# Where an attention group stands among the FFN matmuls of TensorE: behind a second one rather than behind a first

## The chip, the cores and the metric

The kernel runs on one core of a Trainium2 chip. The metric is the device time of one execution in microseconds. The other cores are idle. Some executions take about 195 us instead of 189; they are called slow and left out of every comparison of times.

## The reference

A polysketch attention feeds an FFN with squared ReLU. Cut to what matters:

```python
# q, k, v: (4, 4, 1088, 32) f32;  S1, S2: (8, 32);  w_in: (128, 2048);  w_out: (2048, 128)
def phi(x):                                   # 64 features per position
    a, b = S1 @ x, S2 @ x                     # "sketch", 8 + 8
    return outer(a, b)
kv, z = sum_s phi(k) v, sum_s phi(k)          # per batch and head
x = (phi(q) @ kv) / (phi(q) @ z + 1e-6)       # -> (4 * 1088, 128)
h = max(x @ w_in, 0)                          # first FFN matmul, "mm1"
out = (h * h) @ w_out                         # second FFN matmul, "mm2"
```

## The kernel before

The order of the instructions on each engine is made on the host by a small list scheduler. Each operation has a key (lower is more urgent), the engines that can do it with an estimated duration, and what it depends on. The FFN operations are chained so that they alternate, `mm2(u)`, `mm1(u+4)`, `mm2(u+1)`, and so on; the attention groups of TensorE are put in when they are the most urgent one that is ready.

```python
    def run(self, hop=0.25):
        ...
        t = 0.0
        while todo:
            later, done = [], []
            for e in free:
                ...
                best, wait = None, []
                for op in todo:
                    ...                                   # r: when op is ready for e
                    if r > t:
                        later.append(r)
                        wait.append((r, op["key"]))
                    elif best is None or op["key"] < best["key"]:
                        best = op
                ...
                if best is not None:
                    best["start"], best["eng"] = t, e
                    ...
        for op in sorted(self.ops, key=lambda op: (op["start"], op["n"])):
            op["emit"](op["eng"])
```

What the groups and the FFN matmuls are on TensorE (names as the profile shows them):

```python
    # mm1, "pg<-xT,w_in": F32R, 128x128 of the array, ONE instruction of n columns
    nc.tensor.matmul(st["pg", u][:, n*i : n*i+n], w_in[:, 128*(d0+i) : ...], st[b, "xT"][:, c0 : c0+n])
    # mm2, "po<-g,w_o": f32, 128x128 of the array, TWO instructions of n columns
    nc.tensor.matmul(po[0][:, 0:n], w, g, start=(d == 0), stop=(d == NB - 1))

    # "qc", "kc" (the sketches): 16 tiles of 32x32, f32, so 32 instructions
    def sketch(t_, src, c0, n, w, col=0):
        for h in range(H):
            for c in range(4):
                r = slice(32*h, 32*h + 32)
                nc.tensor.matmul(t_[32*c : 32*c+32, 512*h+col : ...], w[r, :], src[r, c0+n*c : ...])
    # "kvp" (a_kvs): tiles of 128x32, 80 instructions;  "nd" (a_nd): tiles of 32x32, 64 instructions (in batch 0, 16 more of 128x32)
```

## Time and profile before

| | before |
|---|---|
| time, median of 6 runs | 189.32 us (189.06 to 195.55, one slow) |
| span of the profiled run | 187.4 us |
| TensorE on the chain that ended last | 94% |
| busy: PE, PEld, DVE, ACT | 97%, 65%, 61%, 80% |
| waits of TensorE's matmuls after 14.2 us | none listed |
| FFN pair with 384 columns | 0.82 us |

TensorE is the bound, so all that counts is how much time its own instructions take in their order. The useful measure of that is start to start. One caution for reading the timelines: within the steady alternation a pg is recorded as started about 0.3 us before its turn, while the second half of a po still streams (halves of a po start 0.32 us apart; the second half at 64.86 us streams until 65.18, and the next pg is recorded at 64.89). Recorded durations overlap, and only distances between like places are safe. The marks at both ends of what the change can reach, in the timeline of the kernel before, are the first FFN matmul and the last second one (columns: start, duration, engine, line, operation, operands, shape, count):

```profile
14.17 0.47 PE L615 MATMUL pg<-xT,w_in 128*128 128x256 f32 x2 [0.27 <-DVE xT L810]
...
182.28 1.06 PE L648 MATMUL pol<-w_o,g 128*128 128x128 f32 x8
```

They lie 182.28 - 14.17 = 168.11 us apart.

### The profile page before, as it was taken

The page shows a single profiled execution, that of the slowest core. Times are in us where ns is not written, and L with a number is a line of the kernel's source. Part 1 is how long each engine was busy: PE and PEld are TensorE (multiplying, and loading weights), DVE is VectorE, ACT ScalarE, POOL GpSimd, SP SyncE. Part 2 cuts the span into 40 slices and gives each one's busy share as a digit, 9 for nine tenths or more (in the row PEclk, how much of TensorE's full clock was granted, in tenths as well). Part 3 has the DMA queues.
Part 4 walks back from the last instruction along what each step waited for, and adds up shares of the span by engine and source line. Part 5 has one row for each costly group of instructions (what it writes and reads, how often), then busy time and mean ns, then how long its engine had stood idle before and what let it go on. Part 6 is the DMA issues. An engine that isn't in the chain of part 4 may idle for free.

```text
span 187.4 us, 4142 instructions
## 1 busy us (share of the span) xinstructions
PE 182.0 (97%) x1586; PEld 121.8 (65%) x1587; DVE 115.0 (61%) x261; ACT 149.4 (80%) x329; POOL 28.0 (15%) x125
## 2 busy tenths in 40 slices
PE   8999999999999999999999999999999999999991
PEld 2757866666656666656577666656577655666890
DVE  4779879958992589469944589469943412222400
ACT  3418778778978989789698989789698998999960
POOL 2832000028400000085000000085000000000000
PEclk9999999999999999999999999999999999999998
DMA  6799400100039600200069200200020200020101
GB/s 189 189 344 325 125 3 2 28 3 5 0 50 251 143 6 0 44 1 2 7 146 251 35 3 0 42 3 0 7 41 0 35 0 2 9 43 0 31 11 28
DMA packets 24411, 11.27 MB, mean 60 GB/s; under 512 B 17864, under 2 KB 22728, under 8 KB 24392
## 3 DMA queue, kind: packets, MB, share of 16 engines
q1 hardware_dynamic: 23940, 10.82, 23.7%
q8 instruction: 12, 0.20, 0.4%
q10 hardware_dynamic: 452, 0.20, 0.4%
q14 instruction: 7, 0.06, 0.1%
HBM read 8.78 MB, written 2.23 MB: 59 GB/s over the span
## 4 chain that ended last, share of the span: by engine, by line
PE 94%; DMA 2%; DVE 1%; issue 0%; ACT 0%; POOL 0%; ACTq 0%; DVEq 0%
PE po L653 60%; PE pg L615 18%; PE nd L538 3%; PE kvp L394 2%; PE pol L648 2%; PE po L648 2%; PE qc L296 2%; DMA s_nat<-in_S_dram 2%; PE kvp L376 1%; PE kf L306 1%; PE kc L296 1%; PE x L749 1%; PE nd L547 1%; PE den L795 0%; PE den L773 0%
## 5 line engine op out<-in xcount | busy, mean ns | idle before, releaser
L653 PE MATMUL po<-g,w_o 128*128 128x384 f32 (+3 forms) x352 | 138.4, 478 | 0.0
L615 PE MATMUL pg<-xT,w_in 128*128 128x384 f32 (+3 forms) x192 | 110.1, 582 | 0.3 <-DVE xT L810 0.3
L624 ACT ACTIVATE gt<-pg 128x384 f32<-128x384 f32 (+4 forms) x177 | 85.2, 489 | 20.0 <-PE pg L615 16.9
L653 PEld LDWEIGHTS po<-g,w_o 128*128 128x128 f32 x352 | 62.6, 189 | 22.3 <-issue 7.3
L632 ACT ACTIVATE g<-gt 128x384 f32<-128x384 f32 (+3 forms) x138 | 71.0, 532 | 2.9
L615 PEld LDWEIGHTS pg<-xT,w_in 128*128 128x128 f32 x192 | 36.0, 190 | 25.1 <-issue 7.2
L634 DVE TENSOR_TENSOR g<-gt 128x384 f32<-128x384 f32 (+4 forms) x39 | 21.4, 550 | 39.5 <-ACT gt L624 39.4
L443 POOL COPY kv<-kvt 32x64 f32<-32x64 f32 x48 | 11.8, 246 | 89.7 <-PE po L653 63.9
L506 DVE STREAM_SHUFFLE qa<-qc 128x576 f32<-128x576 f32 (+2 forms) x20 | 11.6, 650 | 0.0
L521 DVE TENSOR_TENSOR qp<-qa,qb 128x576 f32<-128x576 f32 (+2 forms) x20 | 10.8, 601 | 0.0
L497 POOL COPY rd<-rc 32x9 f32<-32x9 f32 x48 | 8.9, 185 | 2.2
L347 DVE TENSOR_TENSOR kp<-fs 128x576 f32<-128x576 f32 x12 | 8.2, 741 | 0.0
L469 DVE STREAM_TRANSPOSE qt<-qc 128x576 f32<-128x576 f32 x6 | 4.3, 762 | 5.5 <-PE qc L296 5.5
L657 DVE STREAM_TRANSPOSE oT<-po 128x384 f32<-128x384 f32 (+3 forms) x11 | 6.2, 560 | 1.2 <-PE po L653 1.2
L538 PE MATMUL nd<-qp,kv 32*32 32x288 f32 (+2 forms) x320 | 6.8, 353 | 0.0
L338 DVE STREAM_TRANSPOSE fs<-kc 128x576 f32<-128x576 f32 x6 | 4.3, 762 | 3.9 <-PE kc L296 3.9
L538 PEld LDWEIGHTS nd<-qp,kv 32*32 32x32 f32 x320 | 3.8, 103 | 3.5 <-issue 2.1
L584 DVE TENSOR_TENSOR xT<-nd,bc 128x576 fp32r<-128x576 f32 (+2 forms) x10 | 5.6, 596 | 0.8 <-PE nd L538 0.7
L506 DVE STREAM_SHUFFLE qb<-qc 128x576 f32<-128x576 f32 (+2 forms) x10 | 6.0, 648 | 0.0
L696 PE MATMUL warm<-const-bfloat16-1.0 128*128 128x512 bf16 x12 | 5.2, 585 | 0.8 <-PEq L1072 0.8
L289 DVE STREAM_TRANSPOSE qT<-qn 128x192 f32<-128x192 f32 (+3 forms) x11 | 5.8, 562 | 0.0
L575 DVE STREAM_TRANSPOSE bc<-rd 128x576 f32<-128x576 f32 (+2 forms) x10 | 5.7, 603 | 0.1
(98 smaller groups left out, 97.6 us busy)
## 6 DMA issues: line engine op xcount, KB each, us to landing
kn<-in_k_dram SPq DMA_DIRECT2D x3, 544.0 KB, 6.8
qn<-in_q_dram SPq DMA_DIRECT2D x3, 544.0 KB, 6.7
vn<-in_v_dram SPq DMA_DIRECT2D x9, 144.0 KB, 5.3
out_dram<-oT SPq DMA_DIRECT2D x24, 48.0 KB, 1.8
w_in<-in_moe_w_in_dram SPq DMA_DIRECT2D x4, 256.0 KB, 6.5
w_o<-in_moe_w_out_dram SPq DMA_DIRECT2D x4, 256.0 KB, 5.9
out_dram<-oT SPq DMA_DIRECT2D x8, 56.0 KB, 1.9
qn<-in_q_dram SPq DMA_DIRECT2D x1, 416.0 KB, 5.6
```

Source lines behind the costliest of these rows:

```text
L347: nc.vector.tensor_tensor(out=_ap(st[b, "kp"], 0, 128, 2 * o, [[64, NT], [8, 8], [1, 8]]), in0=_ap(fs, 0, 128, o, [[32, NT], [1, 8], [0, 8]]),
L443: nc.gpsimd.tensor_copy(_ap(st[b, "kv"], 32 * c, 32, 64 * h, [[32, E], [1, 32]]), _ap(st["kvt"], 32 * h, 32, 0, [[64, E], [1, 32]]),)
L497: nc.gpsimd.tensor_copy(st[b, "rd", 0][32 * h : 32 * h + 32, NT * c : NT * c + NT], st[b, "rc"][32 * c : 32 * c + 32, NT * h : NT * h + NT],)
L506: nc.vector.stream_shuffle(in_=banks(st[b, "qc", i0], 2 * x, 0, m), out=_ap(st[b, which, i0], 0, 128, 2 * m * x, [[m, 2], [1, m]]), mask=m ...
L521: nc.vector.tensor_tensor(out=st[b, "qp", i0, e][:, r], in0=st[b, f"qa{e}", i0][:, r], in1=st[b, "qb", i0][:, r], op=mult,)
L538: nc.tensor.matmul(nd[32 * h : 32 * h + 32, 512 * c + col : 512 * c + col + m], kv[r, o : o + 32], qp[r, m * h : m * h + m], start=(e == 0 ...
L615: nc.tensor.matmul(st["pg", u][:, n * i : n * i + n], w_in[:, 128 * (d0 + i) : 128 * (d0 + i) + 128], st[b, "xT"][:, c0 : c0 + n],)
L624: nc.scalar.activation(gt[:, 0:w], st["pg", u][:, 0:w], Relu)
L632: nc.scalar.activation(g2[:, 0:w], gt[:, 0:w], Square)
L634: nc.vector.tensor_tensor(out=g2[:, 0:w], in0=gt[:, 0:w], in1=gt[:, 0:w], op=mult)
L648: nc.tensor.matmul(po[x // 128][:, 0:128], g[:, x : x + 128], w, start=(d == 0), stop=(d == NB - 1),)
L653: nc.tensor.matmul(po[0][:, 0:n], w, g, start=(d == 0), stop=(d == NB - 1))
```

## The change

The intent: an attention group between a first and a second FFN matmul was held to be dearer than one between a second and a first, since a short mm1 seems to hide little of the group's first weight load. So where the last pick was an mm1 and the best is no FFN operation, the best FFN operation that is ready goes first.

```diff
+FFN = ("mm1", "mm2")
...
-        t = 0.0
+        t, last = 0.0, ""
...
-                best, wait = None, []
+                best, wait, can = None, [], []
...
-                    elif best is None or op["key"] < best["key"]:
-                        best = op
+                    else:
+                        can.append(op)
+                        if best is None or op["key"] < best["key"]:
+                            best = op
...
+                if e == "PE" and best is not None and last == "mm1" and best["name"][0] not in FFN:
+                    best = min((op for op in can if op["name"][0] in FFN), key=lambda op: op["key"], default=best)
                 if best is not None:
+                    if e == "PE":
+                        last = best["name"][0]
```

## The prediction

> **What bounds the kernel now.** I read the header of the page first, then the chain of work that ended last, then the waits, and last the timeline of TensorE around single attention groups.
>
> ```profile
> PE 182.0 (97%) x1586; PEld 121.8 (65%) x1587; DVE 115.0 (61%) x261; ACT 149.4 (80%) x329; POOL 28.0 (15%) x125
> ...
> PE 94%; DMA 2%; DVE 1%; issue 0%; ACT 0%; POOL 0%; ACTq 0%; DVEq 0%
> ```
>
> TensorE is on the ending chain for 94% of the 187.4 us. The list of waits has only two for its matmuls, 0.8 us on the sequencer at the start and 0.3 us on the first x; after 14 us none is listed. So every microsecond between 14 and 182 is a matmul streaming or the array changing what it does. A change of order on TensorE can gain only by (a) making such changes cheaper or (b) shortening the two ends. The granted clock is 1.00 in every ten-microsecond stretch up to 180 us, so nothing is to be had from the clock.
>
> Now the unit of work. A first FFN matmul (pg, F32R) is one MATMUL; a second (po, f32) is two. With 384 columns, the timeline reads around one attention group, the sketch kc of batch 2, which stands after a first FFN matmul:
>
> ```profile
> 64.07 0.63 PE L615 MATMUL pg<-xT,w_in 128*128 128x384 f32 x1
> ...
> 64.89 0.63 PE L615 MATMUL pg<-xT,w_in 128*128 128x384 f32 x1
> 65.45 0.77 PE L296 MATMUL kc<-kT,sf 32*32 32x288 f32 x32
> 66.15 0.91 PE L653 MATMUL po<-g,w_o 128*128 128x384 f32 x2
> 66.60 0.63 PE L615 MATMUL pg<-xT,w_in 128*128 128x384 f32 x1
> ```
>
> The pair pg, po has a period of 64.89 - 64.07 = 0.82 us. Around the group the distance from pg to pg is 66.60 - 64.89 = 1.71 us, so the group costs 1.71 - 0.82 = 0.89 us net. The tempting reading: kc starts 0.56 us after pg, where the next po normally starts 0.47 us after it (64.54 - 64.07), and the po after kc lasts 0.91 instead of 0.81: about 0.1 lost going in and 0.1 coming out, "because the short pg hides no weight load". The question is whether the same group after a po loses less. The kernel holds the control: qc of batch 1 has the same shape (32 matmuls of 32x288), and stands after a po:
>
> ```profile
> 40.44 0.63 PE L615 MATMUL pg<-xT,w_in 128*128 128x384 f32 x1
> 40.91 0.81 PE L653 MATMUL po<-g,w_o 128*128 128x384 f32 x2
> 41.65 0.77 PE L296 MATMUL qc<-qT,sw 32*32 32x288 f32 x32
> 42.35 0.47 PE L615 MATMUL pg<-xT,w_in 128*128 128x448 f32 x1
> 42.66 0.81 PE L653 MATMUL po<-g,w_o 128*128 128x384 f32 x2
> 43.01 0.66 PE L615 MATMUL pg<-xT,w_in 128*128 128x448 f32 x1
> ...
> 43.86 0.66 PE L615 MATMUL pg<-xT,w_in 128*128 128x448 f32 x1
> ```
>
> From the pg at 40.44 to the pg at 43.01 are 2.57 us. In them lie one pair with 384 columns in pg (0.82) and one with 448 (43.86 - 43.01 = 0.85). The group costs 2.57 - 0.82 - 0.85 = 0.90 us net. After pg 0.89, after po 0.90: equal to the 0.01 us that two-decimal times allow. The other three sketches after a pg (80.10, 107.64, 122.29 us) show the same 1.71 from pg to pg.
>
> The weight loads say why:
>
> ```profile
> 40.74 0.37 PEld L653 LDWEIGHTS po<-g,w_o 128*128 128x128 f32 x2
> 41.65 0.23 PEld L296 LDWEIGHTS qc<-qT,sw 32*32 32x32 f32 x32 [0.55 <-PE pg L615]
> 42.34 0.19 PEld L615 LDWEIGHTS pg<-xT,w_in 128*128 128x128 f32 x1 [0.47 <-ACT g L632]
> ```
>
> A long po runs before qc, with ample time to hide a load of 0.1 us, and yet the first load of qc starts only at 41.65, as the first matmul of qc does. Half a po streams 0.32 us (the second half before it starts at 41.23 in the trace), so it has streamed out at 41.55, and the load comes 0.09 us later. For kc after pg the same sum gives 0.09 to 0.1 us. Neither kind of FFN matmul hides the entry. The po and pg after the groups likewise begin with a load that nothing covers.
>
> **What the Trainium skill says.** "TensorEngine Tiling (Array Packing)", section Tiling Modes, Key Properties: changing the tiling mode, not merely the tile, drains the TensorE. The groups are 32x32 (sketch, nd) or 128x32 (kvp), the FFN 128x128, so each group pays two changes of mode, whichever neighbour it has. The trace agrees with its 0.09 us on both kinds of entry. "TensorE: Matmul & The Clock Gate", Part 3, The mechanism: a weight load overlaps a matmul in flight only when its row group differs; a 128-row FFN matmul holds all row groups, which fits too. (The same page, Part 2, Step-by-step, adds the background weight buffer, by which FFN loads do hide: the load of po at 64.36 us ran while pg streamed.) No page gives a cost that depends on the matmul before the change.
>
> **The change, part by part.** It is only in the program that orders the instructions. It adds and removes no instruction. When TensorE's last pick was an mm1 and the next best is not FFN, it takes the best FFN operation that is ready, if there is one; in the steady alternation that is an mm2. The fallback means "always" is not strict.
>
> Which picks does it touch? From the start up to 38 us, one group follows a pg: qc at 14.8 us. By the program's constants relu of unit 1, which frees the buffer of the next mm1, ends after qc is ready (1.23 against 1.08 on its clock), so no FFN operation is ready and the fallback leaves it. The other groups there (18.9, 24.3, 28.0, 33.5 us) already follow a po. The first pick that changes is kvp of batch 1 at 38.7 us. In all seven groups follow a pg and precede a po: kvp at 38.7, 77.0 and 119.2; the sketches at 65.5, 80.1, 107.6 and 122.3. Each goes behind the next po, that is, begins about 0.65 us later (the length of a po in the chain of work). The nd groups at 52.7, 91.4 and 133.6 already follow a po.
>
> Cost of the direct part: 4 sketches x (0.90 - 0.89) = 0.04 us or less, slower if anything. For the 3 kvp groups there is no example after a po; their entry after pg looks the same (0.56 us from pg to group: 77.00 - 76.44), and I take 0. Sum: 0.0 us, give or take 0.1.
>
> Indirect part: what waits for those groups gets its input 0.65 us later, and up to one more pair (0.82) where the next group, waiting for w, misses its old slot; 1.5 us together. Against that stands the lead of x. The last xT of batch 1 ends at 55.79 us and its first mm1 starts at 58.78: 3.0 us. For batches 2 and 3 it is 94.45 against 101.71 and 136.65 against 143.91: 7.3 us each. The delay fits into the lead, so no new wait of TensorE follows from it. The po that moves ahead of the group needs its squared g: in the steady alternation it starts at that distance from its mm1 all the time without a wait. Squares may change between ACT and DVE, which are 80% and 61% busy: off the path.
>
> **The rivals.** First, the intent is right and the roughly 0.2 us of entry and exit are saved at each of seven groups: 7 x 0.2 = 1.4 us, giving 188.0. For it: the stretched po (0.91) after the group. Against it: the same 0.90 net in the control, and the same late load. Second, half of that: a pg entry hides something in kvp, which the control doesn't cover: 3 x 0.1 = 0.3 us, 189.1. Third, the later groups delay a chain. ACT gets no new pg while a group runs that stands between po and pg, or a square moves to an engine that is late, and TensorE waits. Such a wait would be a few tenths (the waits of ACT for pg, 16.9 us over 25 times, are slack of 0.7 us each); two or three of them make 190.2. Against it: units run four ahead, and the distance from one mm1 to the next around a group is the same in either order. Fourth, the start is reshuffled after all: xT of chunk 2 ends at 22.37 and its mm1 starts at 22.52, so any delay of qc at 14.8 goes straight into the time, about 1 us, 190.5. Against it: the fallback, as worked out.
>
> **Range and chances.** The runs before were 189.06, 189.63 and 195.55, the profiled one 189.23; leaving out the slow one they average 189.3. With 0.0 from the direct part I predict 189.4. The range has to hold the first rival's milder half and the third: 188.5 to 190.4. Two per cent are 3.8 us, more than all seven groups' entries and exits together, so faster by 2% has 1%; slower by 2% would take a new stall on every batch, 3%.
>
> **What would show it.** Right: the seven groups preceded by po in the timeline; the distance from pg to pg around a sketch still 0.89 to 0.90 above its pairs; still no wait listed for po or pg after 14 us; the same instruction counts; the start identical up to 38.7 us. Wrong: net cost of a sketch near 0.7 us (first rival), new idle time before po or pg with ACT or DVE as its end (third), or qc no longer at 14.8 us (fourth).

## The result, and the profile after

189.38 us (median of 6 runs, 189.12 to 195.44, one slow) against 189.32 us. The ratio of the fast runs is 1.0005, with a 95% interval from 0.9988 to 1.0022: the same. (Ratios here are the mean time of one kernel's fast runs over that of the other's of the same rounds, so not quite the ratio of the medians.) The result was correct.

The profiled run of the changed kernel has a span of 187.7 us. Lines of its page, and its list of TensorE's waits:

```profile
PE 182.4 (97%) x1586; PEld 122.0 (65%) x1587; DVE 114.9 (61%) x260; ACT 149.7 (80%) x330; POOL 28.2 (15%) x125
...
PE 94%; DMA 2%; DVE 1%; issue 0%; ACT 0%; POOL 0%; ACTq 0%; DVEq 0%
```

```profile
PE warm L704 <- PEq L1080: 0.8, 1, 0.8
PE pg L623 <- DVE xT L818: 0.3, 1, 0.3
```

There are the same instructions on TensorE and the same two waits. One square went from DVE to ACT. The program did change: all seven groups now stand behind a po; only qc at the start (15.09 us here) is still behind a pg. This is the timeline of TensorE around the sketch kc of batch 2, and the weight loads there:

```profile
65.15 0.63 PE L623 MATMUL pg<-xT,w_in 128*128 128x384 f32 x1
65.62 0.81 PE L661 MATMUL po<-g,w_o 128*128 128x384 f32 x2
66.36 0.77 PE L304 MATMUL kc<-kT,sf 32*32 32x288 f32 x32
67.06 0.45 PE L623 MATMUL pg<-xT,w_in 128*128 128x384 f32 x1
67.34 0.81 PE L661 MATMUL po<-g,w_o 128*128 128x384 f32 x2
67.69 0.63 PE L623 MATMUL pg<-xT,w_in 128*128 128x384 f32 x1
```

```profile
65.45 0.36 PEld L661 LDWEIGHTS po<-g,w_o 128*128 128x128 f32 x2
66.36 0.23 PEld L304 LDWEIGHTS kc<-kT,sf 32*32 32x32 f32 x32 [0.55 <-PE pg L623]
67.06 0.19 PEld L623 LDWEIGHTS pg<-xT,w_in 128*128 128x128 f32 x1 [0.47 <-ACT g L640]
```

From the pg at 65.15 to the pg at 67.69 are 2.54 us; less two pairs of 0.82 the group costs 0.90 us, against 0.89 where it stood before. Its first load still starts with its first matmul, though a po of 0.64 us was there to hide it. (The releaser named in the bracket had long been done, and is not what held it.) The same sum for kvp of batch 2 from the unrounded starts gives 1.45 us in either kernel; the sketches, unrounded, give 0.895 us before and 0.897 after.

End to end, the first pg and the last pol of the changed kernel:

```profile
182.56 1.06 PE L656 MATMUL pol<-w_o,g 128*128 128x128 f32 x8
```

Its first pg starts at 14.45 us, so the distance is 182.56 - 14.45 = 168.11 us, as before; unrounded it is 168.104 against 168.115. Of the 0.31 us by which the spans differ 0.28 lie ahead of the first pg: the fourteen kf matmuls at 5.3 us take 1.98 us from their first to what follows them, before 1.68 us. The order of the program is the same there. The first clock record of a trace, of the full clock, stands at 5.93 us in this run, so 0.62 us of kf came before it; in the run before it stands at 5.03 us, ahead of kf. Other runs of the experiments below fit: with the record at 6.47 us (late5) kf takes 2.33 us, and with the record ahead of it (full_after_mm2) 1.68. When the record comes varies from run to run, and the change has no part in it.

### The profile page after: what moved, and what is told of

Same layout as the page of the kernel before. It is cut to its first block, busy times and chain, and to the rows that moved or that the text cites. A ratio compares the mean times of both kernels' runs of the same rounds, so it can differ in the third digit from the quotient of the medians.

```text
span 187.7 us, 4140 instructions
## 1 busy us (share of the span) xinstructions
PE 182.4 (97%) x1586; PEld 122.0 (65%) x1587; DVE 114.9 (61%) x260; ACT 149.7 (80%) x330; POOL 28.2 (15%) x125
## 4 chain that ended last, share of the span: by engine, by line
PE 94%; DMA 2%; DVE 1%; issue 0%; ACT 0%; POOL 0%; ACTq 0%; DVEq 0%
PE po L661 59%; PE pg L623 19%; PE nd L546 3%; PE kvp L402 2%; PE pol L656 2%; PE po L656 2%; PE qc L304 2%; DMA s_nat<-in_S_dram 2%; PE kf L314 1%; PE kvp L384 1%; PE kc L304 1%; PE x L757 1%; PE nd L555 1%; PE den L803 0%; PE den L781 0%
## 5 line engine op out<-in xcount | busy, mean ns | idle before, releaser
L623 PE MATMUL pg<-xT,w_in 128*128 128x384 f32 (+3 forms) x192 | 108.8, 575 | 0.3 <-DVE xT L818 0.3
L661 PEld LDWEIGHTS po<-g,w_o 128*128 128x128 f32 x352 | 63.1, 189 | 20.4 <-issue 5.3
```

Of the source, the lines that this page charges most:

```text
L623: nc.tensor.matmul(st["pg", u][:, n * i : n * i + n], w_in[:, 128 * (d0 + i) : 128 * (d0 + i) + 128], st[b, "xT"][:, c0 : c0 + n],)
```

## The experiments

Theory: a group pays for leaving the 128x128 mode of the array and for coming back, whatever stands beside it. Rival: entry after a pg is dearer, and the gain is lost elsewhere. The traces above speak for the theory already; the runs below turn the change round, measure the disputed price alone, and try the other half of the prediction, that lateness of a group costs nothing while x has a lead. All kernels here are edits of the changed one. All results were correct.

**The rule turned round.**

```diff
-                if e == "PE" and best is not None and last == "mm1" and best["name"][0] not in FFN:
-                    best = min((op for op in can if op["name"][0] in FFN), key=..., default=best)
+                if e == "PE" and best is not None and last == "mm2" and best["name"][0] not in FFN:
+                    best = min((op for op in can if op["name"][0] == "mm1"), key=..., default=best)
```

> The rule turned round: an attention group that would follow a second FFN matmul is put behind the next first one. All groups from the qc at 28 us on, thirteen of them (nd and the ones the change moved too), then follow a pg. Theory (a group pays for its two changes of array mode, and the neighbour doesn't matter): the same time as both kernels, within 0.2 us of the changed kernel in the traces from the first moved group to the last matmul, each sketch still 0.89 to 0.90 us net. Rival (entry after a pg costs 0.1 to 0.2 us more): 13 x 0.1 to 0.2 = 1.3 to 2.6 us slower, ratio 1.007 to 1.014.

Measured: 189.23 us (5 runs, none slow), ratio 1.0008 (0.9994 to 1.0021) to the kernel before. Thirteen groups stand behind a pg. The timeline of TensorE at the same kc, and at the last pol:

```profile
64.72 0.63 PE L623 MATMUL pg<-xT,w_in 128*128 128x384 f32 x1
65.28 0.77 PE L304 MATMUL kc<-kT,sf 32*32 32x288 f32 x32
65.98 0.91 PE L661 MATMUL po<-g,w_o 128*128 128x384 f32 x2
66.43 0.63 PE L623 MATMUL pg<-xT,w_in 128*128 128x384 f32 x1
...
182.12 1.06 PE L656 MATMUL pol<-w_o,g 128*128 128x128 f32 x8
```

66.43 - 64.72 = 1.71 us, 0.89 net. The first pg of this run starts at 14.01 us, so the distance to the last pol is 168.11 us for the third time. With seven (before), none (changed) or thirteen (mirror) of these groups behind a pg, the time of TensorE's work agrees to about 0.01 us; the rival had 1.3 to 2.6 us between the two rules.

**The price alone.** Sixteen extra matmuls of 64 columns, with one change of mode in and one out, once behind mm1 and once behind mm2. They write PSUM columns that nothing reads.

```diff
+    def extra(t_, rows, cols):
+        nc.tensor.matmul(t_[0:cols, 384:448], w_o[0:rows, 0:cols], w_o[0:rows, 128:192],
+                         start=False, stop=True, skip_group_check=True)
     ...
         # small_after_mm1, behind the matmul in ffn1:
+        if b in (1, 2) and n == 384 and d0 % 4 == 2:
+            extra(st["pg", u], 32, 32)
         # small_after_mm2, behind the matmul in ffn2:
+            if b in (1, 2) and n == 384 and d0 % 4 == 2:
+                extra(po[0], 32, 32)
```

> One extra 32x32 matmul (64 columns, f32, two passes) behind every fourth first FFN matmul of the four 384-column chunks of batches 1 and 2, 16 in all, into unused columns of the same PSUM tile. Theory: each costs two changes of mode, about 0.3 us, plus 0.11 us of streaming (2 x 64 columns[...]): 0.40 to 0.50 us from pg to pg over the bare 0.82, in all about 7 us. Its first weight load starts about 0.09 us after the pg has streamed out. Rival: 0.1 to 0.2 us more than small_after_mm2.

> The same 16 extra matmuls behind the second FFN matmul. Theory: the same cost as in small_after_mm1 within 0.02 us each. Rival (a long po hides the entry): 0.1 to 0.2 us less each, 1.6 to 3.2 us less in all.

The weight loads of small_after_mm1, then those of small_after_mm2:

```profile
72.62 0.19 PEld L629 LDWEIGHTS pg<-xT,w_in 128*128 128x128 f32 x1
73.20 0.13 PEld L619 LDWEIGHTS pg<-w_o 32*32 32x32 f32 x2 [0.40 <-issue]
73.43 0.30 PEld L669 LDWEIGHTS po<-g,w_o 128*128 128x128 f32 x2
```

```profile
71.99 0.37 PEld L667 LDWEIGHTS po<-g,w_o 128*128 128x128 f32 x2
72.90 0.13 PEld L619 LDWEIGHTS po<-w_o 32*32 32x32 f32 x2 [0.55 <-issue]
73.13 0.19 PEld L629 LDWEIGHTS pg<-xT,w_in 128*128 128x128 f32 x1
```

In both the row of weight loads is empty before the small load (0.40 and 0.55 us), and the small load to the next large one is 0.23 us. In the second, the last half of the po starts at 72.49 us and streams 0.32 us, so the small load at 72.90 comes 0.09 us after it has streamed out. To sum all sixteen I take the distance between the first mm1 of the fourth FFN chunk and that of the tenth, which holds them all:

| kernel | fourth to tenth chunk, us | over the changed kernel, per visit | time, us |
|---|---|---|---|
| before | 85.130 | | |
| changed | 85.132 | | |
| small_after_mm1 | 91.851 | 0.420 | 195.71 |
| small_after_mm2 | 91.838 | 0.419 | 196.04 |
| full_after_mm2 | 88.665 | 0.221 | 192.76 |
| cols_after_mm2 | 91.931 | 0.425 | 195.93 |
| small_twice | 91.944 | 0.426 | (slow profile) |

Behind a pg 0.420, behind a po 0.419 us: the neighbour makes 0.001 us. Of the 0.42 us, 0.11 are streaming (estimated from the 0.32 us of a half po: 2 x 64/384 x 0.32), so a visit pays about 0.31 us around its work. The times of the two, from two runs each, differ by 0.3 us; the traces place that ahead of the first pg again (it starts at 14.05 and 14.32 us).

**The control without a change of mode**: the same, with `extra(po[0], 128, 128)`.

> The control without a change of mode: the extra matmul takes 128 rows and 128 columns of the array, the same 64 moving columns, behind the second FFN matmul. Theory: its first weight load starts while the po before it still streams, 0.3 us ahead of its own matmul, no drain; the cost is set by two loads of 128 columns that 64 columns can't cover, about 2 x 0.18 = 0.36 us. If instead the load starts about 0.09 us after the po has streamed out, as in the small one, then it isn't the mode that delays it.

Its weight loads, then its matmuls:

```profile
71.68 0.51 PEld L619 LDWEIGHTS po<-w_o 128*128 128x128 f32 x2
72.11 0.19 PEld L629 LDWEIGHTS pg<-xT,w_in 128*128 128x128 f32 x1
```

```profile
71.36 0.81 PE L667 MATMUL po<-g,w_o 128*128 128x384 f32 x2
72.00 0.33 PE L619 MATMUL po<-w_o 128*128 128x64 f32 x2
```

The load starts at 71.68, 0.32 us ahead of its matmul at 72.00, and meanwhile the second half of the po streams. So an extra matmul as such does not hold its load back; this one also touches every row of the array, so the row groups are not the reason either. The size was missed: 0.22 us a visit and not 0.36; the first of its two loads is hidden behind the po. The extra with a change of mode costs 0.42 - 0.22 = 0.20 us more than the one without (whose loads are also longer, 0.19 against 0.10 us each).

The unrounded starts, nearly the same in all sixteen visits, divide these sums. After the last half of the po has streamed its 0.32 us, the small extra starts 0.09 us later and the full one at once. Between the two halves of the extra lie 0.080 and 0.055 us. From the second half to the pg are 0.144 and 0.085 us, and from the pg to the next po 0.28 and 0.26 us, where the steady alternation leaves about 0.18 for the pg. Of the 0.20 us, then, about 0.09 are at the entry, 0.03 between the halves and 0.08 at the exit.

**The mode of kvp**: `extra(po[0], 128, 32)`.

> The extra matmul takes 128 rows and 32 columns of the array (the shape of the kvp groups), behind the second FFN matmul. If the change of mode is what costs: the same late first load and the same exit as small_after_mm2, 0.40 to 0.50 us each. If only small row groups cost: no late load, less than 0.3 us.

It costs 0.425 us a visit, as the first of the two branches had it. The number of rows does not matter here; leaving the 128 columns is enough.

**Two extras in one visit**: `extra` twice in a row, the second in rows and columns from 32 on.

> As small_after_mm2, with a second 32x32 extra matmul in another tile of the array right behind the first, so 32 extras in 16 visits. One visit with one extra cost 0.42 us. If a visit's price is the change of mode, the second extra costs only its own work, at most the 0.11 us that it streams, probably less because tiles overlap: 0.42 to 0.53 us a visit, 6.7 to 8.5 us from the first mm1 of chunk 3 to that of chunk 9 over the changed kernel. If each small matmul costs by itself: 0.84 us a visit, 13.4 us.

It costs 0.426 us a visit: the second extra adds 0.007 us. For extras this small the price is one of the visit and not of the matmul. The profile fell in the slow state and the distance above is read from it; its first pg starts at 20.30 us, so what makes it slow lies ahead of that, as the last section shows. The one fast run took 195.87 us.

**Groups held back.** Each kvp group waits for K more pairs after it could go, and all that hangs on it follows.

```diff
+                if e == "PE" and best is not None and best["name"][0] == "kvs":
+                    if n2 < hold.setdefault(best["name"], n2 + K):      # n2: mm2 picked so far
+                        best = min((op for op in can if op["name"][0] in FFN), key=..., default=best)
 ...
```

> The changed kernel with each kvp group held back by two more pairs of FFN matmuls (1.64 us); what hangs on it follows. Lead of the first half of xT of batch 1 in the changed kernel: it ends at 56.33 us, its first mm1 starts at 59.04 us, 2.7 us; 1.64 of them are used. Theory (a delay costs nothing until the lead is used up): same time, within 0.3 us, no wait of TensorE. Rival (lateness costs from the first moment, through busier DVE and ACT): 0.5 us or more slower.

189.24 us (5 runs, one slow), ratio of the fast ones 0.999 (0.997 to 1.001). From the first pg to the last pol 168.13 us against 168.10 unrounded. The profile is of a slow run, but its list of waits has nothing new for TensorE after the first pg.

> Held back by five more pairs (4.1 us). Theory: batch 1 overruns its lead of 2.7 us by 1.4 us, batches 2 and 3 (lead 7.2 us) don't: slower by 1.4 us, between 0.7 and 2, as a wait of TensorE for xT of batch 1 and only there.

190.26 us (4 runs), 1.005 (1.003 to 1.007). First pg to last pol: 169.12 us, 1.0 more. TensorE's waits, beside the two at the start:

```profile
PE pg L627 <- DVE xT L596: 0.9, 1, 0.9
```

One wait, for the xT of batch 1 (its pg starts at 60.46 us), and none in batches 2 and 3. Of the expected 1.4 us 1.0 came. The first half of xT ended 3.84 us later and not 4.1. The lead was 0.3 us longer than counted, because the pg that marks its end is recorded early, and 0.15 us of it, from the end of xT to the pg, can't be used: 3.84 - 2.71 - 0.3 + 0.15 = 0.98 us.

> Held back by eight more pairs (6.6 us). Theory: batch 1 overruns by 6.6 - 2.7 = 3.9 us, batches 2 and 3 still don't: slower by 3.9 us, between 3 and 4.5, ratio about 1.02.

195.35 us (4 runs, none slow), 1.031 (1.027 to 1.036). First pg to last pol 174.22 us: 6.1 more, not 3.9. This is a miss, and the stretches of the trace (columns: stretch, its length, busy time of PE, PEld, DVE, ACT, POOL, then the granted clock) say where it comes from:

```profile
58.00:62.00 4.00, 2.69 (x65) 0.84 (x64) 4.00 (x7) 0.82 (x2) 0.00 (x0) 0.86 0.00 0
62.00:66.00 4.00, 2.94 (x21) 1.66 (x6) 1.95 (x3) 1.01 (x2) 0.00 (x0) 0.50 0.00 0
66.00:70.00 4.00, 4.00 (x13) 2.38 (x11) 1.30 (x3) 2.77 (x6) 0.00 (x0) 0.78 0.02 4
```

While TensorE waited (1.3 us for qp, 1.1 us for xT are listed), its clock fell to half at 60.92 us and came back at 67.75 by the trace's clock records. The distance from the first pg to that of the fourth chunk grew by 4.4 us, of which about 0.3 is the early record of the pg in the changed kernel: 4.1, near the 3.9 expected. The rest of 2.0 comes after it, and from the fourth chunk's first pg at 63.56 us to the return of the clock are 4.2 us at half clock, that is some 2 us lost. The lead explains the wait, and the half clock that follows the wait adds the rest; I had left that out. The times agree: the two runs with a mean granted clock of 0.991 took 194.61 and 194.94 us, the two with 0.982 took 195.76 and 195.87.

## Why the prediction was right

It said 189.4 us, range 188.5 to 190.4, and left 96% for "same" (1% faster, 3% slower); 189.38 was measured, with a ratio of 1.0005.

- **The bound and the groups touched.** Right: the same seven groups moved, the program is unchanged up to 38 us, and qc at 14.8 us stayed where it was, so the fourth rival fell. One reading of the start was wrong without harm: the clock of 1.00 in the first stretch stands for a time that has no clock record up to 5.03 us. Until the record comes the warm-up matmuls start 0.43 us apart; where it comes early (3.46 us, in cols_after_mm2) those after it start 0.22 us apart. So the start had something to gain from the clock, though not by this change.
- **The direct part, "0.0 us, give or take 0.1".** Right: 0.90 against 0.89 us for a sketch, 1.45 for kvp in both, and 168.11 us from the first pg to the last pol in three orders. The single control that was read from the profile of before, a qc behind a po, already spoke against the tempting reading; for kvp the 0 was an assumption, and it held.
- **Why the entry is equal.** The change of mode was named, with the row groups beside it as a second reason "which fits too". The control of full size shows that the row groups are not the reason: a 128-row extra behind a 128-row po was loaded 0.32 us ahead. That part of the argument was not needed, and was wrong as a cause.
- **The indirect part.** Right: the last xT of batch 1 came 56.996 - 55.786 - 0.27 (the later start of the profiled run) = 0.94 us later, those of batches 2 and 3 by 0.68 us, within the 0.65 to 1.5 foreseen and far inside the lead; no wait came of it. The lead itself was measured from the wrong mark: the first mm1 of a batch needs the first half of xT, which ended at 55.12 us for batch 1, so its lead was 3.7 us and not 3.0. The error was on the safe side. Holding kvp back further found the end of the lead where the expectations put it, between two and five pairs for batch 1, and beyond it a cost that was not foreseen in full.
- **The rivals.** The first (1.4 us saved) and the second (0.3) fell with the mirrored rule and the two placements of the extra matmul; the third (new waits) with the list of waits.

What stays open is why the small load waits: the runs show that it does so on leaving the 128 columns, that the pg's load waits likewise on the way back (its load and matmul start together, at 73.13 us in small_after_mm2), and the price, but not what the array does meanwhile.

## What to carry to other kernels

Before moving a piece of work to a "cheaper" place, look in the old profile for one that already stands in such a place, and compare net costs from like mark to like mark; a gap in front of the group and a stretched matmul behind it show that it has a price, not that the price depends on the neighbour. Where matmuls of a few columns in small tiles visit a stream of 128x128 ones, the number of visits is what to reduce: two small matmuls in one visit cost 0.426 us, one cost 0.419. Delay in a chain with a lead is free until the lead is gone, and from there on it can cost more than the wait itself, where the clock falls: it did in late8, after a delay of xT of 6.9 us, and not in late5, after 3.8.

## What the Trainium skill lacked or had wrong

- "TensorEngine Tiling (Array Packing)", Tiling Modes, Key Properties, says that a change of mode drains the TensorE, and gives no price. Here a visit of one small f32 matmul costs 0.42 us, of which 0.11 us are streaming; 0.20 us more than the same extra in the 128x128 mode; equal behind a short F32R matmul and a long f32 one (0.420 and 0.419 us), and equal for tiles of 32x32 and 128x32 (0.419 and 0.425 us).
- "TensorE: Matmul & The Clock Gate", Part 3, The mechanism, says in its list that a weight load overlaps a matmul in flight only when the row group differs. Its own mention of the background weight buffer is the one that holds here: the 128-row extra was loaded 0.32 us ahead, beside a 128-row po.
- The same page, Part 1, What's actually happening, puts the warm-up at about 3.4 us, varying from run to run, and its cost under 1% of a typical span. In the fast profiles here the first record of full clock stands between 3.5 and 6.5 us, that is 2.7 to 5.7 us after the first warm-up matmul. In the two slow profiles it stands at 16.6 and 20.4 us, with the same warm-up matmuls before it. In these the start-up matmuls take 1.8 times as long, for example the first fourteen kf and eight x in late2, against those of before:

```profile
5.33 3.22 PE L318 MATMUL kf<-sf,kt 128*128 128x64 f32 x14
8.48 2.08 PE L761 MATMUL x<-qT,sq 64*128 64x256 f32 x8
```

```profile
5.32 1.75 PE L306 MATMUL kf<-sf,kt 128*128 128x64 f32 x14
7.00 1.13 PE L749 MATMUL x<-qT,sq 64*128 64x256 f32 x8
```

  The first pg comes at 19.29 instead of 14.17 us, and from there to the last pol both take the same 168.1 us: a late rise of the clock, worth 5.1 us or 2.7%. The other, of small_twice, shows the same, with its first pg at 20.30 us. The slow runs of the kernel before and of the changed one (195.55 and 195.44 us) have no profile. Why the clock is late in some runs no experiment here tried.
- The same page's advice (Why this matters for your kernels) is to avoid idle gaps over about 3 us. In late8 the clock fell to half after shorter ones: the last po before them starts at 57.47 us, nd follows at 59.32 after an idle gap of 1.3 us, with six scattered matmuls up to 60 us, and the fall is at 60.92.
